# The last 64 contraction rows of two experts: full 128-row products in place of row pairs

## The chip, the cores and the metric

The kernel runs on one core of a Trainium2 chip. The metric is the device time of one execution in microseconds. Three runs of the kernel before gave 1248.62, 1251.45 and 1251.56 us, so its median is 1251.45 us.

## The reference, cut to what matters

A recurrent attention (4 batches, 8 heads, 768 steps, width 40) feeds two experts over 3072 tokens of width 320. All of it is float32:

```python
x = attn_out.transpose(0, 2, 1, 3).reshape(B * S, H * D)      # 3072 x 320
h = x @ w_in                                                  # 320 -> 2048
x = (h * (1.0 / (1.0 + np.exp(-1.702 * h)))) @ w_out          # 2048 -> 320
a, b = x @ w1, x @ w2                                         # 320 -> 1024, twice
y = ((a * b) @ w3) @ w_out2                                   # 1024 -> 1024 -> 320
```

The contractions over 320 in `x @ w_in`, `x @ w1` and `x @ w2` are what the change is about: 320 is two times 128 and a rest of 64.

## The kernel before, in words

The tensor engine multiplies float32 numbers that are split in a high part and a remainder (the tiles ending in h and l). A product of two such numbers is taken as high times high, high times low and low times high. For the first 256 contraction rows that makes three products of 128 rows for each of two row blocks. For the last 64 rows one tile holds the high parts on one half of the partitions and the low parts on the other half (`wir` and `wr` for the weights; `xt4`, `xt5` and `xtb4`, `xtb5` for the tokens, which hold the halves in opposite order). One full 128-row product of `wir` with the opposite tile gives the two mixed terms at once. The high times high term is a product over 64 rows alone, `wir[r]` with `X(4 + h)[r]`.

So each output tile of 128 features takes eight products: six full ones, one full mixed one and one of 64 rows. The kernel before places the 64-row product of one feature tile last and that of the next one first, on the other half of the partitions and into another PSUM bank, so that two stand next to each other on the engine.

The first expert (`moe1`, 12 blocks of 256 tokens) makes 16 feature tiles per block: line 895 emits the eight products (256 columns each), lines 899 to 902 apply the activation and split the result, and line 876 (in `l2`) emits the six products of 320 columns with the output weights, two feature tiles behind. The second expert (`moe2`, 6 blocks of 512 tokens) makes 8 pairs of feature tiles per block: line 1078 emits two times eight products of 512 columns, lines 1083 to 1087 multiply and split, and line 1061 (in `l4`) emits twelve products of 320 columns. Line 1013 folds w3 into the last output weights beforehand.

The attention (lines 381 to 671) is a chain of small products of 32 to 104 rows with work on VectorE, ScalarE and GpSimd between them. A block of the first expert can start when four groups of the attention are done.

The order of all instructions is made before the kernel runs, by `Plan.run`: a list schedule that takes operations as they become ready, by their `at` (their turn) and an assumed cost. It assumes 0.1095 us for each product of line 895, and 0.2155 us for each of line 1078, whatever their rows. Each engine then runs its list strictly in that order. Products of the experts ("PEw") alternate with those of the attention. In the first expert an extra key, "m1", on the first and last product of each feature tile keeps the two 64-row products adjacent.

Of the kernel before, what the change touches and what calls it, by code (L numbers as in the profile page):

```python
# [9 lines left out]
F32 = mybir.dt.float32  # L10
# [8 lines left out]
C = 64            # chunk length  # L19
NB = 4            # batches  # L20
NP = 4            # head pairs
D = 40
NCH = 12
NG = NCH * NB     # groups: one chunk of one batch
NBLK = 6          # token blocks of two chunks
TB = 512
DM = 320
# of a group, per head: the whole chunk's product of decays, those to the chunk's end, those from its start, a, b
# [4 lines left out]
NF = 256          # tokens of a block of the first expert: one chunk  # L33
NLW = 3
NLE = 7           # first loads in the room of the weights to come
NCV = 40 + 20     # tiles of weights taken to float32 before the last expert's output weights
LAG = 2           # its second product runs behind the first
OWN = {"PE": 0.0, "DVE": 0.127, "ACT": 0.13, "Pool": 0.1}     # latency to the next one on the same engine, us
# [34 lines left out]
LE = 4          # first products of a and b emptied by the scalar engine  # L73
JA = 4          # first masked products of a and k left to the others than the vector engine
PMIN = 1e-20       # below 0.5 ** 64: no product of decays within the guards is so small
# [7 lines left out]
class Bank:  # L83
    """A PSUM bank, bound to a tile when its first writer is emitted."""
# [5 lines left out]
class Plan:  # L90
    """Operations in a plain sequential order, emitted in the order of a list schedule.

    Every operation names what it reads and writes; that gives the order that has to
    stay, the rest is free: each engine takes, of what is ready, the operation whose
    turn `at` comes first.
    """
# [40 lines left out]
    def run(self, log=None):  # L137
# [6 lines left out]
        # a bank is taken only when what empties it waits for nothing older  # L144
# [18 lines left out]
        warm, win, act = False, 0, 0.0      # the clock of the tensor engine  # L163
# [69 lines left out]
def rwkv_moe_kernel(ctx: ExitStack, tc: tile.TileContext, LA, JK, JR, KBT, VT,  # L233
# [8 lines left out]
    x2sc = dp.tile([NCH, 2, 128, DM], F32, name="x2sc")    # transposed within blocks of 32 x 32  # L242
    psc = dp.tile([NG, 104, SC], F32, name="psc")
    w12sc = dp.tile([8, 3, 128, 256], F32, name="w12sc")
    G_X = 16 + 4 * NBLK            # columns of GD: inputs, T, x, weights
# [13 lines left out]
    # constants  # L259
# [39 lines left out]
    # ------------------------------------------------------------ turns  # L299
# [14 lines left out]
    # ------------------------------------------------------------ set-up  # L314
# [53 lines left out]
    # ------------------------------------------------------------ attention  # L368
# [17 lines left out]
    def L_part(n):  # L386
        at = at_L(n)
        if n < NLE:           # the first ones in the room of the weights to come
            t, nm = le[n], f"le{n}"
        else:  # L390
            m = (n - NLE) % (NLW + 1) if n < 16 else (n - 16) % NLW
            t, nm = (lw[m], f"lw{m}") if m < NLW else (xsg[0:104, 0:SC + 256], "lx")
# [25 lines left out]
        # what is not below the diagonal is left out later  # L418
# [9 lines left out]
    def T_part(blk):  # L428
# [12 lines left out]
        # all rows for the second diagonal blocks, then the first ones over it  # L441
# [6 lines left out]
        def upper():  # L448
            """Zeros over the diagonal, ones on it; the steps below keep under it."""
            for h in (16, 8, 4, 2, 1):  # L450
                g.memset(bass.AP(LP.tensor, lpf[:, h:].offset, [list(lpf.ap[0]), [66 * h, 16 // h], [32, h], [1, h]]), 0.0)
            g.memset(lpf[:, 0:1024:33], 1.0)
# [15 lines left out]
        # what the merges need first; what the first diagonal blocks' rows get here the merges write over  # L468
# [128 lines left out]
    def S_part(n):  # L597
# [5 lines left out]
        if n >= 4:  # L603
            # the state times all of the chunk's decay, and its transpose
# [73 lines left out]
    # ------------------------------------------------------------ weights  # L678
# [23 lines left out]
    def f64(at, n, srcs):  # L702
        """Tile of float32 from float64 words, all 24 bits; a guard counts the results that are normal."""
# [35 lines left out]
    def split(at, dst_h, dst_l, src, key, kd, n=256, eng="Pool", r=()):  # L739
        """Exact halves of src; kd: key of the result."""  # L740
# [5 lines left out]
    def remainder(at, dst, st, key, kd, h):  # L746
        """High parts of rows 64h to 64h + 63 of st on the same rows of dst, the low parts on the other rows."""
# [44 lines left out]
    # ---- first expert  # L792
    xrc = [0]

    def x_part(blk, at, second):
        """The tokens of a block in exact halves."""
# [63 lines left out]
    def moe1(k):  # L860
# [19 lines left out]
        for f in range(16):  # L880
# [7 lines left out]
            r = slice(64 * h, 64 * h + 64)  # L888
            prods.append((lambda fs=fs: wir[:, fs], lambda h=h: X(5 - h)))
            # half of the rows: next to that of a neighbour, which is on the other rows  # L890
            prods.insert(7 * (f % 2), (lambda fs=fs, r=r: wir[r, fs], lambda h=h, r=r: X(4 + h)[r]))
            for i, (a, b) in enumerate(prods):
                if i == 7 and f % 2 and f >= LAG:
                    l2(f - LAG)
                op("PEw", 0.1095, at(), lambda a=a, b=b, i=i, B=B: mm(B.t[:, 0:NF], a(), b(), start=(i == 0), stop=(i == 7)),  # L895
                   r=ks + [f"wi{f // 2}"], w=[B] + ["m1"] * (i in (0, 7)))
# [7 lines left out]
            if f >= LAG and f % 2 == 0:  # L904
                l2(f - LAG)
# [8 lines left out]
    # ---- second expert  # L914
    order2 = [(k % 2) * 4 + k // 2 for k in range(8)]

    def second_weights():
        """w1 and w2 as float32 in DRAM: piece c, rows k."""
# [122 lines left out]
    def moe2(blk):  # L1041
# [12 lines left out]
        def l4(f):  # L1054
            gi = f % 2
            terms = [(t, z, *("gh gh gl".split()[z], "ph pl ph".split()[z])) for t in range(4) for z in range(3)]
            if f == 7:      # the low parts are the last to come
                terms.sort(key=lambda x: (x[0] // 2, x[1] // 2, x[0]))
# [5 lines left out]
        for f in range(8):  # L1064
            gi = f % 2
            Bs = []
            for m in range(2):
# [5 lines left out]
                prods.append(("wr", None, 5 - m))  # L1073
                prods.insert(7 - 7 * m, ("wr", None, 4 + m))
                r = slice(64 * m, 64 * m + 64)
                for i, (a, k, b) in enumerate(prods):
                    rows = r if k is None and b == 4 + m else slice(0, 128)
                    op("PEw", 0.2155, at(), lambda a=a, k=k, b=b, i=i, B=B, fs=fs, rows=rows: mm(  # L1078
                        B.t, dyn[a][rows, fs] if k is None else dyn[a][:, k, fs], X(b)[rows], start=(i == 0), stop=(i == 7)),
# [13 lines left out]
        for t in range(4):  # L1093
# [6 lines left out]
            q = s if t % 2 and blk == NBLK - 1 else sp       # two queues at the very end  # L1100
# [4 lines left out]
    # ------------------------------------------------------------ input guards  # L1105
    def guards():
        """Decays within (0.5, 1.5), b not large; the first expert's weights make room."""
# [27 lines left out]
    def verdict():  # L1135
        """How many of the guards hold."""
# [13 lines left out]
    # ------------------------------------------------------------ program  # L1150
# [40 lines left out]
    # the general path computes everything again when a guard does not hold  # L1191
# [6 lines left out]
def general_path(ctx: ExitStack, tc, ysc, rr, rk, rv, rw, ra, rb, w_in, w_out, w1, w2, w3t, w_o2, out):  # L1198
    """Step by step over time, then both experts in plain float32: for inputs outside the guards."""
# [82 lines left out]
    # w3 comes transposed: fold it into the output weight, rows of w3 along the free side  # L1282
# [46 lines left out]
def host(inputs):  # L1329
# [3 lines left out]
    def hp(x):  # L1333
        x = x.reshape(NB, NP, 2, NCH, C, D)[:, :, ::-1]
        return x.transpose(2, 5, 3, 0, 1, 4)  # eo e c b hp t
# [6 lines left out]
    def rows(*xs):      # the odd heads on rows 0 to 39, the even ones on rows 64 to 103  # L1342
# [6 lines left out]
    LA[D:64, :, NP * C + 1:2 * NP * C:C] = 2.0 ** -40      # the unused rows fade  # L1349
    JR = f(H["r"])  # L1350

    def tm(x):
        x = x.reshape(NB, NP, 2, NCH, C, D)
        return x.transpose(3, 0, 4, 1, 2, 5).reshape(NG, C, NP, 2, D)  # n s p eo' d (0 = even)
# [6 lines left out]
    VT = v.transpose(0, 1, 3, 2, 4)  # n s eo' p d  # L1361
# [32 lines left out]
```

## Time and profile before

| | |
|---|---|
| median of three runs | 1251.45 us |
| span of the profiled execution | 1251.8 us |
| PE busy | 1078.5 us (86%), 11322 matmuls |
| weight loads (PEld) busy | 915.3 us (73%) |
| DVE, ACT, POOL busy | 818.6, 697.8, 508.8 us |
| mean granted TensorE clock | 0.946 of full speed |
| first and last product of the first expert's input (line 895) | start at 170.9 and 958.9 us |
| last attention product (line 664) | starts at 787.4 us |
| last product of the second expert (line 1061) | starts at 1232.5 us |

The page gives no time of the profiled execution other than its span. Busy time of PE counts a product from its start to its modelled end, and products overlap in the array: a 256-column product lasts about 0.28 us, while the next one starts after about 0.115 us. What a product costs is therefore read from the distance between starts, not from its duration.

### The profile page before, as it was taken

To read this page: it belongs to the slowest core of one execution; us is meant where nothing else is said; L and a number is where in the kernel's file an instruction comes from. 1 tells how busy PE (TensorE), PEld (TensorE's weight loads), DVE (VectorE), ACT (ScalarE), POOL (GpSimd) and SP (SyncE) were. 2 spreads that over 40 slices of the span, in tenths; PEclk is the share of its full clock that TensorE was granted. 3 is DMA by queue.
4 is the path that set the end of the run, shared out by engine and by line. 5 is a ranking of instruction groups with operands and counts; after the bars stand their busy time and mean duration, and the time that the engine had idled before them with its cause. 6 is when DMAs were issued, how large, how long until landed. Compare 5 with 4: busy or idle time off the path is not lost.

```text
span 1251.8 us, 30058 instructions
## 1 busy us (share of the span) xinstructions
PE 1078.5 (86%) x11322; PEld 915.3 (73%) x11322; DVE 818.6 (65%) x1571; ACT 697.8 (56%) x2050; POOL 508.8 (41%) x704
## 2 busy tenths in 40 slices
PE   3355678788997989898998999999999999999993
PEld 3244467676876778777877788999998778878873
DVE  8999999989869996996589323577742233233221
ACT  4345576775675666564755677687754933223121
POOL 4546654766456646543654454454432000000000
PEclk9999978888899989887998999999999999999997
DMA  7537554765476447433632333344324621021000
GB/s 216 147 96 206 150 150 107 187 178 132 121 199 185 122 131 209 124 94 86 159 91 62 90 86 75 85 143 129 121 55 88 224 47 28 19 47 27 4 21 24
DMA packets 187017, 139.71 MB, mean 112 GB/s; under 512 B 123632, under 2 KB 157680, under 8 KB 186864
## 3 DMA queue, kind: packets, MB, share of 16 engines
q1 hardware_dynamic: 186604, 137.38, 41.2%
q8 instruction: 91, 1.49, 0.5%
q14 instruction: 62, 0.51, 0.1%
q10 hardware_dynamic: 260, 0.33, 0.1%
HBM read 107.82 MB, written 29.83 MB: 110 GB/s over the span
## 4 chain that ended last, share of the span: by engine, by line
PE 46%; DVE 3%; DMA 1%; ACT 1%; issue 1%; POOL 0%; SPq 0%; DVEq 0%; POOLq 0%; ACTq 0%
PE bank L1078 15%; PE bank L895 9%; PE bank L876 8%; PE bank L1061 7%; PE bank L1013 2%; PE bank L663 1%; DVE lp L463 1%; PE bank L637 1%; PE bank L648 1%; DVE tmp L459 1%; PE bank L536 1%; DMA lw<-in_LA_dram 0%; DVE lp L443 0%; PE bank L626 0%; DMA pq<-psc 0%
## 5 line engine op out<-in xcount | busy, mean ns | idle before, releaser
L902 POOL TENSOR_TENSOR gl<-xsg,gh 128x256 fp32r<-128x256 f32 x192 | 152.3, 795 | 152.7 <-ACT gh L901 104.1
L895 PE MATMUL bank<-xt,wih 128*128 128x256 f32 x768 | 166.7, 303 | 0.0
L895 PEld LDWEIGHTS bank<-xt,wih 128*128 128x128 f32 x768 | 126.0, 196 | 12.8 <-issue 1.3
L876 PE MATMUL bank<-woh,gh 128*128 128x320 f32 x384 | 125.8, 328 | 3.2 <-DVE xo L911 3.2
L899 ACT ACTIVATE xsg<-bank 128x256 f32<-128x256 f32 x192 | 73.6, 384 | 94.4 <-PE bank L895 91.2
L876 PE MATMUL bank<-woh,gl 128*128 128x320 f32 x384 | 124.6, 325 | 0.0
L876 PE MATMUL bank<-wol,gh 128*128 128x320 f32 x384 | 124.6, 324 | 0.0
L1084 DVE TENSOR_TENSOR sa<-bank,sa 128x512 f32<-128x512 f32 x48 | 33.2, 692 | 138.6 <-PE bank L1078 134.9
L895 PE MATMUL bank<-xt,wil 128*128 128x256 f32 x384 | 112.3, 293 | 0.0
L895 PE MATMUL bank<-xt,wir 64*128 64x256 f32 (+1 forms) x384 | 103.4, 342 | 0.8 <-ACT xsg L899 0.8
L463 DVE TENSOR_TENSOR lp<-lp,tmp 128x30 f32<-128x30 f32 (+9 forms) x180 | 89.1, 495 | 4.3
L574 POOL TENSOR_TENSOR xy<-xy,mup 64x256 f32<-64x256 f32 x96 | 78.9, 822 | 27.8 <-ACT xy L572 20.2
L459 DVE TENSOR_TENSOR tmp<-lp 128x30 f32<-128x30 f32 (+9 forms) x180 | 82.3, 457 | 3.9
L663 PE MATMUL bank<-xy,kb 128*40 128x104 f32 x384 | 56.7, 300 | 27.9 <-DVE xy L654 27.8
L876 PEld LDWEIGHTS bank<-woh,gh 128*128 128x128 f32 x384 | 75.4, 196 | 6.7 <-DVE xo L911 3.6
L901 ACT CAST gh<-xsg 128x256 fp32r<-128x256 f32 x192 | 77.2, 403 | 3.0
L895 PEld LDWEIGHTS bank<-xt,wir 64*128 64x128 f32 (+1 forms) x384 | 61.6, 193 | 23.3 <-issue 17.0
L876 PEld LDWEIGHTS bank<-woh,gl 128*128 128x128 f32 x384 | 75.2, 196 | 3.3 <-issue 1.1
L876 PEld LDWEIGHTS bank<-wol,gh 128*128 128x128 f32 x384 | 75.5, 197 | 2.9 <-issue 0.8
L895 PEld LDWEIGHTS bank<-xt,wil 128*128 128x128 f32 x384 | 75.5, 197 | 1.9 <-issue 0.6
L654 DVE TENSOR_TENSOR xy<-bank,mtx 64x416 f32<-64x416 f32 x96 | 56.4, 587 | 29.4 <-PE bank L649 27.0
L1083 ACT COPY sa<-bank 128x512 f32<-128x512 f32 x48 | 28.2, 587 | 84.8 <-PE bank L1078 84.8
(208 smaller groups left out, 3510.4 us busy)
## 6 DMA issues: line engine op xcount, KB each, us to landing
lw<-in_LA_dram SPq DMA_DIRECT2D x39, 416.0 KB
psc<-lw SPq DMA_DIRECT2D x39, 313.6 KB
pq<-psc SPq DMA_DIRECT2D x48, 209.6 KB
jk<-in_JK_dram SPq DMA_DIRECT2D x48, 208.0 KB
raw<-in_w3t_dram SPq DMA_DIRECT2D x32, 256.0 KB
kb<-in_KBT_dram SPq DMA_DIRECT2D x48, 160.0 KB
raw<-in_w_out_dram SPq DMA_DIRECT2D x20, 256.0 KB
xq<-x2sc SPq DMA_DIRECT2D x72, 64.0 KB
```

The source lines that it names most:

```text
L459: e.tensor_tensor(t, _bc(LP[:, j + 1:32, j:j + 1], [128, n, j]), _bc(LP[:, j:j + 1, 0:j], [128, n, j]), op=ALU.mult)
L463: e.tensor_tensor(LP[:, j + 1:32, 0:j], LP[:, j + 1:32, 0:j], t, op=ALU.add)
L574: op("Pool", 0.69, at, lambda eo=eo, r=r: g.tensor_tensor(xy[r, :, eo, D:104], xy[r, :, eo, D:104], _bc(mup[r], [64, NP, C]), op=ALU.mult) ...
L654: op("DVE", 0.5, at, lambda eo=eo, r=r: v.tensor_tensor(xy[r, :, eo, :], v3(B2, 416)[r], _bc(mtx[r], [64, NP, 104]), op=ALU.mult), r=[B2, ...
L663: mm(ps[64:104, p], kbf[:, 80 * p + 40:80 * p + 80], xy[:, p, 0], start=True, stop=True)
L876: op("PEw", 0.136, at(), lambda w_=w_, g_=g_, z=z, t=t: mm(acc[t].t[:, 0:DM], g_()[:, 128 * t:128 * t + 128], w_(), start=(f == 0 and z == 0),
L895: op("PEw", 0.1095, at(), lambda a=a, b=b, i=i, B=B: mm(B.t[:, 0:NF], a(), b(), start=(i == 0), stop=(i == 7)), r=ks + [f"wi{f // 2}"], w= ...
L899: op("ACT", 0.34, at(), lambda B=B, si=si: s.activation(sg[:, si], B.t[:, 0:NF], AF.Gelu_apprx_sigmoid), r=[B], w=[f"sg{si}"])
L901: op("ACT", 0.305, at(), lambda GH=GH, si=si: s.copy(GH(), sg[:, si]), r=[f"sg{si}"], w=[kg[0]])
L902: op("Pool", 0.69, at(), lambda GH=GH, GL=GL, si=si: g.tensor_tensor(GL(), sg[:, si], GH().bitcast(F32), op=ALU.subtract), r=[f"sg{si}", k ...
L1061: op("PEw", 0.136, at(), lambda a=a, b=b, t=t, ts=ts, z=z: mm(acc[t].t[:, 0:DM], dyn[a][gi][:, ts], dyn[b][:, f], start=(f == 0 and z == 0 ...
L1078: op("PEw", 0.2155, at(), lambda a=a, k=k, b=b, i=i, B=B, fs=fs, rows=rows: mm(B.t, dyn[a][rows, fs] if k is None else dyn[a][:, k, fs], X ...
```

## The change

The 64-row product becomes a product over all 128 rows of the same two tiles. It then also adds low times low on the other 64 rows, which is a term more of the exact product. The two products with `wir` (or `wr`) stand last in every feature tile, none stands first, the "m1" key is gone, and `l2` follows every feature tile instead of standing before the last product of the odd ones. The number of instructions stays the same. Apart from this the diff takes comments away, by which lines move: 895 is now 892, 1013 is 1010, 1061 is 1058, and 1078 is 1072.

```diff
             h = f // 2 % 2
-            r = slice(64 * h, 64 * h + 64)
-            prods.append((lambda fs=fs: wir[:, fs], lambda h=h: X(5 - h)))
-            prods.insert(7 * (f % 2), (lambda fs=fs, r=r: wir[r, fs], lambda h=h, r=r: X(4 + h)[r]))
+            for z in (4 + h, 5 - h):
+                prods.append((lambda fs=fs: wir[:, fs], lambda z=z: X(z)))
             for i, (a, b) in enumerate(prods):
-                if i == 7 and f % 2 and f >= LAG:
-                    l2(f - LAG)
                 op("PEw", 0.1095, at(), lambda a=a, b=b, i=i, B=B: mm(B.t[:, 0:NF], a(), b(), start=(i == 0), stop=(i == 7)),
-                   r=ks + [f"wi{f // 2}"], w=[B] + ["m1"] * (i in (0, 7)))
+                   r=ks + [f"wi{f // 2}"], w=[B])
...
-            if f >= LAG and f % 2 == 0:
+            if f >= LAG:
                 l2(f - LAG)
...
-                prods.append(("wr", None, 5 - m))
-                prods.insert(7 - 7 * m, ("wr", None, 4 + m))
-                r = slice(64 * m, 64 * m + 64)
+                prods += [("wr", None, 4 + m), ("wr", None, 5 - m)]
                 for i, (a, k, b) in enumerate(prods):
-                    rows = r if k is None and b == 4 + m else slice(0, 128)
-                    op("PEw", 0.2155, at(), lambda a=a, k=k, b=b, i=i, B=B, fs=fs, rows=rows: mm(
-                        B.t, dyn[a][rows, fs] if k is None else dyn[a][:, k, fs], X(b)[rows], start=(i == 0), stop=(i == 7)),
+                    op("PEw", 0.2155, at(), lambda a=a, k=k, b=b, i=i, B=B, fs=fs: mm(
+                        B.t, dyn[a][:, fs] if k is None else dyn[a][:, k, fs], X(b), start=(i == 0), stop=(i == 7)),
                        r=ks + [("w2", 4 * m + f // 2)], w=[B])
```

On PE, in the first expert behind the end of the attention, the kernel before has this order from the full mixed product of an odd feature tile (bank 5) to the next tile (bank 4). The sizes are those of the output, so the 64-row products don't show by them: they are the `xt4` product of bank 5 and the `xt5` product of bank 4.

```order
L895 MATMUL bank5_125<-xt5_158,wir_135 128x256
L876 MATMUL bank6_126<-woh_136,gh1_162 128x320
L876 MATMUL bank6_126<-wol_405,gh1_162 128x320
L876 MATMUL bank6_126<-woh_136,gl1_164 128x320
L876 MATMUL bank7_127<-woh_136,gh1_162 128x320
L876 MATMUL bank7_127<-wol_405,gh1_162 128x320
L876 MATMUL bank7_127<-woh_136,gl1_164 128x320
L895 MATMUL bank5_125<-xt4_157,wir_135 128x256
L895 MATMUL bank4_124<-xt5_158,wir_135 128x256
L895 MATMUL bank4_124<-xt0_153,wih_134 128x256
```

In the changed kernel the same place of the program reads:

```order
L892 MATMUL bank5_125<-xt1_154,wil_404 128x256
L892 MATMUL bank5_125<-xt5_158,wir_135 128x256
L892 MATMUL bank5_125<-xt4_157,wir_135 128x256
L876 MATMUL bank6_126<-woh_136,gh0_161 128x320
L876 MATMUL bank6_126<-wol_405,gh0_161 128x320
L876 MATMUL bank6_126<-woh_136,gl0_163 128x320
L876 MATMUL bank7_127<-woh_136,gh0_161 128x320
L876 MATMUL bank7_127<-wol_405,gh0_161 128x320
L876 MATMUL bank7_127<-woh_136,gl0_163 128x320
L892 MATMUL bank4_124<-xt0_153,wih_134 128x256
```

The second product with `wir` moved ahead of the six output products, next to the first, and the next feature tile begins with a full product.

On PE, in the second expert, the kernel before has at the joint of a pair of feature tiles (banks 0 and 2):

```order
L1078 MATMUL bank0_120<-xtb1_11180,w2l_9515 128x512
L1078 MATMUL bank0_120<-xtb5_11184,w2r_9516 128x512
L1078 MATMUL bank0_120<-xtb4_11183,w2r_9516 128x512
L1078 MATMUL bank2_122<-xtb5_11184,w2r_9516 128x512
L1078 MATMUL bank2_122<-xtb0_11179,w2h_9514 128x512
```

The third and fourth rows are the two 64-row products. The changed kernel has there (banks 3 and 0):

```order
L1072 MATMUL bank3_123<-xtb1_11180,w2l_9553 128x512
L1072 MATMUL bank3_123<-xtb4_11183,w2r_9554 128x512
L1072 MATMUL bank3_123<-xtb5_11184,w2r_9554 128x512
L1072 MATMUL bank0_120<-xtb0_11179,w2h_9552 128x512
L1072 MATMUL bank0_120<-xtb2_11181,w2h_9552 128x512
```

The second tile's product with `w2r` left the joint for the end of its own tile.

On PE, right behind the last attention product (line 664), the kernel before goes on with

```order
L664 MATMUL bank3_123<-xy2_94,kb2_97 40x104
L895 MATMUL bank4_124<-xt0_153,wih_134 128x256
L895 MATMUL bank4_124<-xt2_155,wih_134 128x256
L895 MATMUL bank4_124<-xt0_153,wil_404 128x256
L895 MATMUL bank4_124<-xt1_154,wih_134 128x256
```

and the changed kernel with

```order
L664 MATMUL bank1_121<-xy2_94,kb2_97 40x104
L892 MATMUL bank4_124<-xt1_154,wil_404 128x256
L892 MATMUL bank4_124<-xt5_158,wir_135 128x256
L892 MATMUL bank4_124<-xt4_157,wir_135 128x256
L876 MATMUL bank6_126<-woh_136,gh0_161 128x320
```

The first expert's work moved forward against the attention: ahead of the last attention product stand 961 products of line 895 and 708 of line 876 before, and 981 and 720 now, of 1536 and 1152 in all.

## Rows read from the trace of the kernel before

**Rows 1.** Windows, whole core: stretch, length, busy us (count) of PE, PEld, DVE, ACT, POOL; clock, DMA, GB/s

```profile
170.00:577.00 407.00, 351.04 (x4795) 297.94 (x4792) 360.10 (x685) 261.95 (x829) 232.95 (x314) 0.90 0.56 146
577.00:700.00 123.00, 111.78 (x1574) 95.71 (x1574) 86.93 (x166) 71.44 (x225) 61.40 (x88) 0.92 0.40 101
700.00:790.00 90.00, 89.40 (x1242) 77.02 (x1240) 27.97 (x62) 60.96 (x193) 45.26 (x68) 0.98 0.30 74
790.00:960.00 170.00, 170.00 (x1182) 156.82 (x1181) 100.28 (x211) 121.24 (x391) 77.54 (x103) 1.00 0.36 102
960.00:1235.00 275.00, 272.84 (x1359) 217.88 (x1357) 85.65 (x137) 97.31 (x168) 0.74 (x1) 1.00 0.20 55
```

**Rows 2.** Waits of PE, 170 to 700 us, longest: who, for whom, total us, times, longest

```profile
PE bank L663 <- DVE xy L654: 19.8, 8, 4.6
```

**Rows 3.** Timeline of PE, a pair in the first expert: start us, us, engine, instruction, count

```profile
911.23 0.28 PE L895 MATMUL bank<-xt,wih 128*128 128x256 f32 x1
...
911.57 0.31 PE L876 MATMUL bank<-woh,gh 128*128 128x320 f32 x1
...
912.30 0.31 PE L876 MATMUL bank<-woh,gl 128*128 128x320 f32 x1
912.54 0.38 PE L895 MATMUL bank<-xt,wir 64*128 64x256 f32 x2
...
913.19 0.31 PE L1013 MATMUL bank<-foh,f3h 128*128 128x320 f32 x1
```

**Rows 4.** Timeline of PE, a 64-row product alone in the first expert

```profile
929.89 0.31 PE L876 MATMUL bank<-woh,gh 128*128 128x320 f32 x1
930.13 0.38 PE L895 MATMUL bank<-xt,wir 64*128 64x256 f32 x1
930.44 0.41 PE L876 MATMUL bank<-wol,gh 128*128 128x320 f32 x1
930.69 0.31 PE L876 MATMUL bank<-woh,gl 128*128 128x320 f32 x1
```

**Rows 5.** Timeline of PE, a pair in the second expert (the first row merges three products)

```profile
1102.90 0.83 PE L1078 MATMUL bank<-xt,w2r 128*128 128x512 f32 x3
...
1104.23 0.40 PE L1078 MATMUL bank<-xt,w2l 128*128 128x512 f32 x1
...
1104.93 0.39 PE L1078 MATMUL bank<-xt,w2l 128*128 128x512 f32 x1
```

**Rows 6.** Chain that ended last, 1105 to 1112 us: start, us, piece

```profile
1107.33 3.88 PE bank L1078 x16
```

**Rows 7.** Groups of PE by form, 64-row products: 170 to 700, 700 to 790, 790 to 960

```profile
L895 PE MATMUL bank<-xt,wir 64*128 64x256 f32 x99 | 26.5, 400 | 0.8 <-ACT xsg L899 0.8
L895 PE MATMUL bank<-xt,wir 64*128 64x256 f32 x22 | 5.2, 390 | 0.0
L895 PE MATMUL bank<-xt,wir 64*128 64x256 f32 x71 | 16.8, 381 | 0.0
```

**Rows 8.** Windows of line 895 (577, 790), then of line 876: PE, PEld; clock, DMA, GB/s

```profile
577.00:700.00 123.00, 37.95 (x194) 28.67 (x194) 0.92 0.40 101
790.00:960.00 170.00, 90.04 (x564) 73.78 (x562) 1.00 0.36 102
577.00:700.00 123.00, 30.49 (x145) 23.58 (x145) 0.92 0.40 101
790.00:960.00 170.00, 77.18 (x420) 63.43 (x420) 1.00 0.36 102
```

**Rows 9.** Chain that ended last, 577 to 700 us: shares of the stretch by line

```profile
by line: PE bank L895 12.0%; DVE lp L463 8.6%; PE bank L876 8.3%; issue 6.7%; DVE tmp L459 6.0%; DMA lw<-in_LA_dram 4.6%; DVE lp L443 4.4%; DMA pq<-psc 3.7%; DVE ls L475 3.6%; DVE xy L654 3.3%; PE bank L663 3.1%; PE bank L637 2.9%; PE bank 
```

**Rows 10.** Windows, whole core, before and in a stretch at half clock

```profile
570.00:577.00 7.00, 4.57 (x89) 3.83 (x83) 6.91 (x6) 3.88 (x12) 3.31 (x5) 0.93 0.32 84
577.00:600.00 23.00, 23.00 (x293) 20.24 (x294) 8.26 (x20) 11.71 (x35) 7.66 (x12) 0.72 0.37 91
```

**Rows 11.** Waits of ACT, 844 to 930 us

```profile
ACT f3h L976 <- PE bank L1013: 3.9, 3, 1.9
```

## The prediction

> **What bounds the kernel now.** I read the windows first, then the waits and the chain, and last the timeline of PE around the products that change. The windows show two regimes [rows 1]. From 790 to 960 us PE is busy 170.00 of 170.00 us, from 960 to 1235 us 272.84 of 275.00, and from 700 to 790 us 89.40 of 90.00; DVE is busy a third to 60% of these stretches. PE alone sets the pace there, so a microsecond taken from it is a microsecond off the end. From 170 to 700 us PE is idle 56 + 11.2 = 67 us and DVE is busy 84% of the time. PE waits there for the attention, above all line 663 for DVE [rows 2]. In the only part of this stretch that the chain covers, 577 to 700 us, the first expert's products (lines 895 and 876) hold 12.0% + 8.3% = 20.3%, which is 25.0 of 123 us [rows 9]. They are busy for 37.95 + 30.49 = 68.4 us there [rows 8]. So 25.0 / 68.4 = 0.365 of their time lies on the path before 700 us, and all of it afterwards.
>
> **What a pair costs now.** Products are priced by the distance of their starts. Between 911.23 and 911.57 us stand three 256-column products, 0.34 / 3 = 0.114 us each, and from there to 912.30 five of 320 columns, 0.73 / 5 = 0.146 each [rows 3]. The pair of 64-row products starts at 912.54: 0.24 us behind a 320-column product, where 0.146 is normal. From 912.30 to 913.19 there are one 320-column product, the pair and two 256-column ones, 0.89 us. All full they would take 0.146 + 4 x 0.114 = 0.602. So a pair costs 0.29 us more than the two full products that replace it. I take 0.28. The two halves do start together (both lie in one 0.38 us). What is lost is a gap ahead of them and a slow restart behind.
>
> A 64-row product alone is worse. From 929.89 to 930.69 us stand a 320-column product, the single and another 320-column one, 0.80 us. Full they would take 2 x 0.146 + 0.114 = 0.406, so the excess is 0.39 us [rows 4].
>
> In the second expert a full product of 512 columns takes (1104.93 - 1104.23) / 3 = 0.233 us. From 1102.90 to 1104.23 there are a full one, the pair and two full ones, 1.33 us against 5 x 0.233 = 1.167, an excess of 0.16 us [rows 5]. A piece of 16 products with one pair lasts 3.88 against 16 x 0.233 = 3.73, an excess of 0.15 [rows 6]. I take 0.155.
>
> The full product that comes in is not a new price: the mixed product on the same tiles (`wir`, 128 rows) already is one of those three between 911.23 and 911.57 us.
>
> A rule speaks against the change. The Trainium skill (TensorEngine Tiling (Array Packing), Theoretical Speedup) gives up to 2x for a contraction of 64 rows or fewer, since two tiles work at once. By that alone two full products would cost one product more than a pair, and the sum would turn positive (the last rival). The common start of the two halves agrees with it. But the same page says under Key Properties that changing the tiling mode drains the engine, and the gaps around the pair [rows 3 to 5] are what such a drain would look like: 0.28 us lost against 0.114 us won.
>
> **The sum.**
> - 790 to 960 us: 71 products of 64 rows [rows 7]. In the timeline 27 pairs (first at 791.09, last at 955.92 us) and 17 singles make them up: 27 x 0.28 + 17 x 0.39 = 14.2 us. Cross-check by counts [rows 1, 8]: 564 products of 256 columns, 420 + 192 of 320 and 6 of 512 would take 64.3 + 89.4 + 1.4 = 155.1 us in a stretch of 170.0, an excess of 14.9.
> - 700 to 790 us: 22 of them [rows 7], 6 pairs and 2 singles among wide products (2.5 us), and 3 pairs and 2 singles with an attention product on one side, where the array changes its shape anyway. For these I count what is left on the other side, 0.18 and 0.2 us: 0.9. Together 3.4 us.
> - 960 us to the end: 8 pairs in each of 6 blocks; 46 stand as pairs and 4 as singles: 46 x 0.155 + 4 x 0.39 = 8.7 us.
> - 170 to 700 us: 99 of them [rows 7]: 30 pairs and 13 singles among wide products, 4 pairs and 18 singles beside the attention: 13.5 + 4.3 = 17.8 us of PE time. The bounds are 0 (all of it becomes waiting for DVE) and 17.8 (PE sets the pace). I take the share on the chain: 0.365 x 17.8 = 6.5 us.
> - The new order puts 20 products of 256 columns and 12 of 320 more ahead of the last attention product: 20 x 0.114 + 12 x 0.146 = 4.0 us of work that leaves the PE-bound end. It costs nothing where it fills PE's waits, and delays the attention by as much where it lies on the path. The same share gives a gain of 0.635 x 4.0 = 2.5 us, with bounds 0 and 4.0.
> - `l2` behind every feature tile and the freed "m1" key add no instruction and no wait to any other engine or queue; they act by the order alone, which is counted. Activation and splitting keep their work, and DVE has 41% or more and ACT 29% or more to spare where PE is the bound, but for the ACT of rival 4.
>
> After 700 us that is 26.3 us, with the rest 35.3. The profiled span of 1251.8 us (no other time of that execution is given) becomes 1216.5. The median of the runs is 0.35 us below that span, so I predict **1216 us**.
>
> **The rivals.**
> 1. *The time before 700 us gives nothing*: every microsecond that PE saves there is spent waiting for DVE, and the reordering helps nothing. For it: DVE at 84%, PE's waits [rows 1, 2]. Against it: the chain share of 0.365 [rows 9]. 1251.8 - 26.3 = 1225.5 us. Chance 0.18.
> 2. *All of it counts*: PE's queue holds up the attention more than the chain from 577 us shows, and 17.8 + 4.0 us are won there. 1251.8 - 48.1 = 1203.7 us. Chance 0.14.
> 3. *The clock takes part of it back.* Before 700 us the granted clock is 0.90 and 0.92 [rows 1], so about 81 + 20 = 101 us run at 1.2 instead of 2.4 GHz. One such stretch came after PE had been busy for only 4.57 of 7.00 us [rows 10]. More idle time may mean more of them: the 11 us of saving off the path would add a sixth to PE's 67 us of idle time, so 17 us at half clock, 8 us of PE work, some 3 us on the path and at most 8. That is 1219 to 1225 us, chance 0.04. To cancel everything it would take 70 us more at half clock; that is "no change", chance 0.02.
> 4. *The preparation of the second expert's weights becomes the bound* from 844 to 930 us, where line 1013 consumes tiles that ACT, DVE and POOL make. Half of the 14.2 us would turn into waits: 1224 us. Against it: ACT waits there for PE to free a tile, 3.9 us [rows 11], so the preparation is held back by PE. Chance 0.03.
> 5. *Slower: the gaps don't belong to the 64-row products*, but to the joint between two feature tiles, with its new bank. Then they stay, and each pair's second product costs its full 0.114 or 0.233 us: after 700 us 36 x 0.114 + 46 x 0.233 = 14.8, before it 34 x 0.114 x 0.365 = 1.4. That is 1268 us. It decides once a joint keeps more than 0.28 us in the first expert and 0.155 in the second. Against it: the single in rows 4 has the gap on both sides in the middle of a run of output products. Chance 0.03. This is also the time by the skill's 2x rule alone.
>
> **How the numbers follow.** The forecast has 0.56. Faster by over 0.3% (3.8 us, about what a measurement of this kernel can tell from no change) are the forecast and rivals 1, 2, 4 and the mild form of 3: 0.95. Same is 0.02, slower 0.03. The range from 1206 to 1230 us holds the forecast, rivals 1, 4 and the mild 3, and the upper edge leaves 4 us for an attention that the new order delays; rival 2 is partly below it.
>
> **What would show it.** Line 892 follows itself and line 876 without gaps, 0.114 and 0.146 us apart, at every joint; a piece of 16 products of line 1072 lasts 3.73 instead of 3.88 us, and the weight loads' idle time there is gone. The last attention product starts some 4 to 10 us earlier than 787.4, and the distance from it to the end shrinks from 464 to about 437 us. PE's waits before 700 us grow by about 9 to 12 us. If the joints still show 0.24 us entries, the price of a pair was read wrongly; if the distance from 790 us on shrinks as said and the end doesn't follow, the attention was delayed.

## The result and the profile after

The changed kernel takes 1221.4 us (median of 4 runs, 1217.65 to 1223.97) against 1251.51 us before in the same session. The ratio is 0.9767, with a 95% interval of 0.974 to 0.9794: 30 us less. The prediction was 1216 us, with a range from 1206 to 1230.

The page of the changed kernel begins with the span and the busy times of the engines:

```profile
span 1222.2 us, 30059 instructions
PE 1031.5 (84%) x11322; PEld 922.7 (75%) x11322; DVE 820.5 (67%) x1571; ACT 696.9 (57%) x2050; POOL 508.3 (42%) x704
```

The number of products is the same as before. PE is busy for 47 us less, although 288 products now work on twice the rows; the weight loads are busy for 7 us more. The windows, in the columns of [rows 1] and over the same stretches but for the last, which ends with PE's work:

```profile
170.00:577.00 407.00, 339.12 (x4665) 298.07 (x4663) 349.86 (x676) 257.98 (x818) 226.82 (x310) 0.89 0.55 144
577.00:700.00 123.00, 110.48 (x1726) 98.39 (x1726) 97.63 (x175) 78.13 (x244) 63.70 (x93) 0.97 0.44 111
700.00:790.00 90.00, 87.96 (x1280) 79.33 (x1275) 28.07 (x61) 61.88 (x192) 47.20 (x69) 1.00 0.30 73
790.00:960.00 170.00, 169.61 (x1233) 166.33 (x1232) 109.35 (x223) 131.54 (x405) 79.63 (x100) 1.00 0.47 130
960.00:1203.00 243.00, 242.91 (x1255) 212.22 (x1254) 77.73 (x126) 82.12 (x147) 0.00 (x0) 1.00 0.15 42
```

PE is still the bound from 700 us on: it is idle for 2.0, 0.4 and 0.1 us in the last three stretches. From 790 to 960 us it starts 1233 products instead of 1182 [rows 1], in the same 170 us. Before 700 us it now idles 530 - 449.6 = 80.4 us, where it was 67.2. So part of what was saved there became waiting. How much is not firm: a second trace of the changed kernel, taken in the comparison of the orders below, idles 530 - 455.66 = 74.3 us there.

The timeline of PE at a joint of the first expert, which answers to [rows 3]:

```profile
913.12 0.28 PE L892 MATMUL bank<-xt,wil 128*128 128x256 f32 x1
913.23 0.31 PE L876 MATMUL bank<-woh,gl 128*128 128x320 f32 x1
913.38 0.28 PE L892 MATMUL bank<-xt,wir 128*128 128x256 f32 x1
913.49 0.31 PE L876 MATMUL bank<-woh,gh 128*128 128x320 f32 x1
913.64 0.28 PE L892 MATMUL bank<-xt,wir 128*128 128x256 f32 x1
913.75 0.31 PE L876 MATMUL bank<-wol,gh 128*128 128x320 f32 x1
```

Both products with `wir` last 0.28 us like any other, and the next product follows after 0.11 us. The 0.24 us entry and the 0.31 us exit of [rows 3, 4] are gone, even where the two lines alternate product by product. And at a joint of the second expert, which answers to [rows 5]:

```profile
1103.43 0.40 PE L1072 MATMUL bank<-xt,w2l 128*128 128x512 f32 x1
...
1104.13 0.39 PE L1072 MATMUL bank<-xt,w2l 128*128 128x512 f32 x1
1104.36 0.63 PE L1072 MATMUL bank<-xt,w2r 128*128 128x512 f32 x2
1104.83 0.63 PE L1072 MATMUL bank<-xt,w2h 128*128 128x512 f32 x2
```

From 1103.43 to 1104.83 us there are six products, 1.40 / 6 = 0.233 us each, across the joint as well. The weight loads follow each other there without idle time, where they idled 0.37 and 0.25 us around the pair before. In the chain of waits a piece of 16 products now lasts 3.72 us, where [rows 6] had 3.88:

```profile
1108.61 3.72 PE bank L1072 x16
```

Where the time came from can be split at the last attention product (line 664). The row of its line gives durations in ns, then the start of its first and of its last product. The last one started at 787.4 us before:

```profile
L664 PE MATMUL bank<-xy,kb x384: 250/253/396, 90.5 to 784.4; 128*40 128x104 f32 x192
```

From there to the end it was 464.4 us and is 1222.2 - 784.4 = 437.8, so 26.6 us came from behind the attention and 3.0 from before its end. The first number holds in the second trace (26.2 us). The second is less firm: the last attention product starts 4.9 us earlier in the second trace, and 5.5 us earlier in a third one whose program is the same up to the second expert (at 781.9 us, in the run with a 64-row product alone).

### The profile page after: what moved, and what is told of

Its sections match the earlier page's. It is cut to its first block, busy times and chain, and to the rows that moved or that the text cites. A ratio compares the mean times of both kernels' runs of the same rounds, so it can differ in the third digit from the quotient of the medians.

```text
span 1222.2 us, 30059 instructions
## 1 busy us (share of the span) xinstructions
PE 1031.5 (84%) x11322; PEld 922.7 (75%) x11322; DVE 820.5 (67%) x1571; ACT 696.9 (57%) x2050; POOL 508.3 (42%) x704
## 4 chain that ended last, share of the span: by engine, by line
PE 51%; DVE 31%; DMA 6%; issue 6%; ACT 3%; POOL 1%; SPq 1%; DVEq 0%; POOLq 0%; ACTq 0%
PE bank L1072 14%; PE bank L892 9%; PE bank L876 9%; PE bank L1058 7%; DVE lp L463 5%; DVE tmp L459 5%; DMA lw<-in_LA_dram 4%; DVE lp L443 2%; DVE xy L654 2%; PE bank L1010 2%; DVE tt L470 2%; DVE ls L475 1%; DVE st L729 1%; PE bank L663 1%; PE bank L637 1%
## 5 line engine op out<-in xcount | busy, mean ns | idle before, releaser
L892 PEld LDWEIGHTS bank<-xt,wih 128*128 128x128 f32 x768 | 132.8, 199 | 6.7 <-ACT xsg L896 3.9
L892 PE MATMUL bank<-xt,wir 128*128 128x256 f32 x384 | 86.9, 293 | 0.2 <-DVE xt L850 0.2
L574 POOL TENSOR_TENSOR xy<-xy,mup 64x256 f32<-64x256 f32 x96 | 76.8, 800 | 23.6 <-ACT xy L572 16.1
L463 DVE TENSOR_TENSOR lp<-lp,tmp 128x30 f32<-128x30 f32 (+9 forms) x180 | 83.5, 464 | 4.2
L654 DVE TENSOR_TENSOR xy<-bank,mtx 64x416 f32<-64x416 f32 x96 | 56.5, 589 | 26.9 <-PE bank L649 14.5
L588 ACT COPY ivt<-bank 64x208 f32<-64x208 f32 x192 | 62.6, 326 | 20.9 <-PE bank L583 15.0
L1080 ACT CAST gh<-sa 128x512 fp32r<-128x512 f32 x48 | 29.7, 619 | 74.4 <-DVE sa L1078 74.4
L671 POOL TENSOR_TENSOR yh<-yh,pq 104x256 f32<-104x256 f32 x48 | 40.0, 833 | 72.7 <-DVE yh L669 61.4
```

The source lines that it names most:

```text
L463: e.tensor_tensor(LP[:, j + 1:32, 0:j], LP[:, j + 1:32, 0:j], t, op=ALU.add)
L574: op("Pool", 0.69, at, lambda eo=eo, r=r: g.tensor_tensor(xy[r, :, eo, D:104], xy[r, :, eo, D:104], _bc(mup[r], [64, NP, C]), op=ALU.mult) ...
L588: op("ACT", 0.24, at, lambda h=h, d=d: s.copy(ivt[d:d + 64, h // 64::2], B2.t[h:h + 64, 0:208].rearrange("p (a b) -> p a b", a=2)), r=[B2] ...
L654: op("DVE", 0.5, at, lambda eo=eo, r=r: v.tensor_tensor(xy[r, :, eo, :], v3(B2, 416)[r], _bc(mtx[r], [64, NP, 104]), op=ALU.mult), r=[B2, ...
```

## The experiments

All runs have the kernel before beside them on the same chip. My theory: the price lies in the change of the array's shape around each 64-row product. From 700 us on it comes off the end in full, and before that only in part. The rivals were that the gaps belong to the joints between feature tiles, and that the new order made the gain.

### The rows alone, in the old order

The kernel before, every engine's order unchanged, and only the rows raised:

```diff
-            r = slice(64 * h, 64 * h + 64)
+            r = slice(0, 128)
...
-                r = slice(64 * m, 64 * m + 64)
+                r = slice(0, 128)
```

> The kernel before with its own order of instructions on every engine, unchanged, and only the rows of the 64-row products of both experts raised to 128. Theory (the price lies in the change of the array's shape at each 64-row product, and PE sets the pace from 700 us on): 14.2 + 3.4 + 8.7 = 26.3 us less after 700 us, and 0 to 6.5 us less before it: 1219 to 1225 us. Rival (the gaps belong to the joint between feature tiles, and the gain of the change came from its new order): no change, 1248 to 1252 us. What is left between this kernel and the changed one (1221.4 us) is the effect of the new order alone; the prediction had 2.5 us of gain for it.

Measured: 1225.44 us against 1251.34, a ratio of 0.9785 (0.9753 to 0.9817), 26 us less. The rows alone make most of the gain, with the joints and their new banks where they were. In the chain of waits the piece of 16 lasts what it lasts in the changed kernel:

```profile
1107.90 3.72 PE bank L1078 x16
```

The gaps therefore belong to the 64-row products. From the last attention product (785.3 us) to the end of this span (1226.6) it is 441.3 us, 23.1 less than before; the terms behind 790 us had 14.2 + 8.7 = 22.9. The saving ahead of that is small, though 17.8 us of PE time were saved before 700 us. The window from 170 to 700 us shows where it went:

```profile
170.00:700.00 530.00, 444.94 (x6367) 393.41 (x6363) 450.85 (x854) 332.91 (x1053) 292.91 (x401) 0.91 0.52 136
```

PE is busy for 17.9 us less than before in the same stretch (351.04 + 111.78 = 462.8 [rows 1]), with practically the same count of products, 6367 against 6369, and DVE for as long as before. The waits of PE for DVE to empty the first expert's sums grew (the first row is the kernel before, the second this one):

```profile
PE bank L876 <- DVE xo L911: 3.2, 2, 1.6
PE bank L876 <- DVE xo L911: 9.1, 3, 5.2
```

Those for the attention's DVE work at line 663 are longer too, in this trace:

```profile
PE bank L663 <- DVE xy L654: 24.4, 11, 4.9
```

They were 19.8 us before [rows 2]. In a second trace of the same kernel the first wait is 8.2 us and the second 20.9, so the growth at line 663 is not sure.

### The three parts one by one

The same edit, in the first expert's blocks 0 to 5 only (`r = slice(0, 128) if k < 6 else ...`):

> As the first, but full rows only in the first expert's blocks 0 to 5, which run before about 683 us; everything else as before, in the same order. It measures the term of the time before 700 us by itself (17.8 us of PE time). Theory of the prediction (the chain's share, 0.365): 6.5 us less, 1245 us. Rival 1 (all of it turns into waits for DVE): no change, 1251 us. Rival 2 (all of it counts): 1234 us.

Measured: 1248.45 us (12 runs, 1242.78 to 1254.78) against 1251.34, a ratio of 0.9976 (0.9955 to 0.9998): 2.9 us less, and between 0.3 and 5.6 by the interval. It is neither nothing nor the 6.5 us of the prediction, and a third of the full saving at most. Its trace has the last attention product at 778.2 us of 1242.6, so 464.4 us behind it as before: what it saves lies ahead of the attention's end.

In blocks 6 to 11 only:

> As the first, but full rows only in the first expert's blocks 6 to 11, which run from about 683 us on. Theory: 14.2 + 3.4 = 17.6 us less, 1234 us, with the last attention product some 3 us earlier. Rival (joints): no change. Rival (the preparation of the second expert's weights becomes the bound from 844 us on): about 7 us of it missing, 1241 us, and waits of PE for line 978's tiles.

Measured: 1235.83 us, 0.9874 (0.9845 to 0.9903): 15.5 us less, with 17.6 inside the interval (12 to 19 us). The rival of a late preparation would have given 10.6, and PE's waits from 700 to 960 us are these two rows:

```profile
PE bank L895 <- ACT xsg L899: 0.5, 1, 0.5
PE bank L876 <- DVE xo L911: 0.2, 1, 0.2
```

No tile of the preparation (line 978) is among them, so that rival falls. In this trace the last attention product starts at 780.5 us, 6.9 us earlier where 3 were expected (two traces of one kernel differ there by up to 3.6 us, as the comparison of the orders shows), and 1231.4 - 780.5 = 450.9 us stand behind it, 13.5 less than before, where the sum had 14.2.

In the second expert only:

> As the first, but full rows only in the second expert. Theory: 46 pairs at 0.155 and 4 singles at 0.39 us, 8.7 us less, 1242.8 us, and nothing different before 945 us. Rival (joints): no change. Rival (two 64-row products at once are worth one product's time): 46 x 0.233 = 10.7 us more, 1262 us.

Measured: 1242.66 us, 0.9912 (0.988 to 0.9945): 8.7 us less, as the sum had it (7 to 15 us by the interval). Its trace has 1242.4 - 787.9 = 454.5 us behind the last attention product, 9.9 less than before. The rivals (no change, and 10.7 us more) fall. The three parts give 2.9 + 15.5 + 8.7 = 27.1 us, which is what they give together (26) within the intervals.

### A 64-row product alone, away from the joint

The changed kernel, with one of the eight products in each tile of the second expert over 64 rows again:

```diff
                 for i, (a, k, b) in enumerate(prods):
+                    rows = slice(64 * m, 64 * m + 64) if i == 6 else slice(0, 128)
```

(and `rows` used for both operands of the product).

> The changed kernel, but in the second expert the high times high product is over 64 rows again, alone, as the seventh of its tile's eight products, in the middle of the tile and not at a joint: 96 singles. Theory (each change of the array's shape costs): 96 x 0.39 = 37.4 us more than the changed kernel, 1259 us, all of it between 940 us and the end, and gaps of 0.32 us ahead of each. Rival (the gaps belong to the joints between tiles and their new bank): 1221 us.

Measured: 1260.33 us, 1.0062 of the kernel before (1.004 to 1.0084), which is 38.9 us more than the changed kernel. Timeline of PE around one of them (the second row merges the 64-row product with the full one behind it), then the chain's piece of 16 products with two of them:

```profile
1101.93 0.40 PE L1073 MATMUL bank<-xt,w2l 128*128 128x512 f32 x1
1102.26 0.93 PE L1073 MATMUL bank<-xt,w2r 64*128 64x512 f32 x2
1103.02 0.62 PE L1073 MATMUL bank<-xt,w2h 128*128 128x512 f32 x2
```

```profile
1107.19 4.49 PE bank L1073 x16
```

The product enters 0.33 us behind its neighbour instead of 0.233, and it and the next one take 0.76 instead of 0.47. Two singles lengthen the piece by 4.49 - 3.72 = 0.77 us, 0.385 each, in the middle of a tile and in one bank. With 96 of them that is 37 us, more than the whole change won.

So a single takes 0.233 + 0.385 = 0.62 us of PE's time. A pair in the kernel before takes 2 x 0.233 + 0.155 = 0.62 us as well. The second half of a pair costs nothing more; what is paid is the way from 128 rows to 64 and back, once for each single or pair.

The weight loads show where the gaps begin:

```profile
1101.70 0.19 PEld L1073 LDWEIGHTS bank<-xt,w2l 128*128 128x128 f32 x1
1102.26 0.18 PEld L1073 LDWEIGHTS bank<-xt,w2r 64*128 64x128 f32 x1 [0.37 <-issue]
1102.68 0.19 PEld L1073 LDWEIGHTS bank<-xt,w2r 128*128 128x128 f32 x1 [0.24 <-issue]
```

The load for the full product of 1101.93 us starts 0.23 us ahead of it, while the product before still runs. The load for the 64-row product starts with that product, at 1102.26 us. Whether the array has to run empty first, or the load is only not taken ahead where the rows change, these runs don't tell apart.

### The effect of the order

Twice the changed kernel was compared with the rows-only kernel. The second time they ran side by side:

> The changed kernel once more, next to the following one on the same chip. 1221 us. The difference of the two is the effect of the new order alone.

> The kernel before in its own order with full rows in both experts, once more. If the new order gains what the prediction had for it: 2.5 us more than the changed kernel, 1224 us. If it only moves work about: the same as the changed kernel within a microsecond.

Measured: 1219.48 us (0.9747, 0.9716 to 0.9778) and 1225.10 us (0.9806, 0.9773 to 0.9839). The first time it was 1221.4 and 1225.44 us. So the new order is worth 4 to 6 us on top of the rows. The intervals overlap in both sessions, so the times alone don't settle it. The rows of line 664 in the second session, the changed kernel first, help:

```profile
L664 PE MATMUL bank<-xy,kb x384: 250/253/397, 90.5 to 782.5; 128*40 128x104 f32 x192
L664 PE MATMUL bank<-xy,kb x384: 250/253/397, 90.7 to 781.7; 128*40 128x104 f32 x192
```

Their spans are 1220.7 and 1223.0 us. Behind the last attention product the changed kernel has 437.8 and 438.2 us in its two traces, and the rows-only kernel 441.3 us in both. The order is worth 3.1 to 3.5 us there, for 4.0 us of work moved ahead. The attention's end (784.4 and 782.5 us against 785.3 and 781.7) shows no delay that is clear of the difference between two traces of one kernel.

### How much of PE's idle time can be filled

The list schedule of the changed kernel, with other numbers. The first of them has the measured distances as costs:

```diff
-                op("PEw", 0.1095, at(), ...
+                op("PEw", 0.114, at(), ...
```

(0.136 became 0.146 and 0.2155 became 0.233 in the same way.)

> The changed kernel, with the list schedule told the measured distances: 0.114, 0.146 and 0.233 us for products of 256, 320 and 512 columns in place of 0.1095, 0.136 and 0.2155. Its order then has 61 products of line 892 and 48 of line 876 fewer ahead of the last attention product, 61 x 0.114 + 48 x 0.146 = 14 us of work that moves behind it. Theory (0.365 of the experts' work before 700 us lies on the path): attention 5 us earlier, 14 us more behind it, 1230 us. If such work costs the attention nothing: 1235 us. If PE sets the pace of the attention too: 1221 us.

Measured: 1229.55 us, 0.9835 (0.9798 to 0.9873), as the theory gave. But it gave it for the wrong reason, as the row of line 664 shows:

```profile
L664 PE MATMUL bank<-xy,kb x384: 250/253/397, 90.3 to 772.8; 128*40 128x104 f32 x192
```

The attention ends 11.6 us earlier than in the changed kernel (9.7 earlier than in its second trace), not 5, and from there to the end it is 1228.4 - 772.8 = 455.6 us, 17.8 more instead of 14.

The other three change one line:

```diff
-RATIO = 1.25
+RATIO = 1.0
```

> The changed kernel, with RATIO 1.0 in place of 1.25 in the list schedule (the experts get a larger share of PE's turns): 1177 products of line 892 and 865 of line 876 stand ahead of the last attention product, where the changed kernel has 981 and 720. That moves 196 x 0.114 + 145 x 0.146 = 43.5 us of work ahead of it; PE was idle for 82 us from 170 to 790 us. Theory (0.365 of it on the path): the attention ends 16 us later and the end comes 28 us earlier, 1194 us. If PE sets the pace of the attention: 1221 us. If PE's waits take it all: 1178 us.

Measured: 1246.22 us, 0.9965 (0.9948 to 0.9982). The expectation was far off.

```profile
L664 PE MATMUL bank<-xy,kb x384: 250/253/397, 90.4 to 817.7; 128*40 128x104 f32 x192
```

```profile
170.00:790.00 620.00, 537.34 (x7608) 482.30 (x7605) 472.89 (x897) 399.99 (x1260) 342.53 (x475) 0.94 0.49 127
790.00:960.00 170.00, 150.58 (x1203) 141.49 (x1203) 107.05 (x226) 132.75 (x403) 73.78 (x97) 0.94 0.48 141
```

```profile
PE bank L1072 <- ACT xtb L837: 11.7, 2, 11.0
PE bank L1072 <- DVE xtb L849: 5.5, 1, 5.5
```

The attention ends 33.3 us later. PE's idle time from 170 to 790 us is 82.7 us, what it was (80.4 + 2.0). The products that moved ahead did not fill a wait; they moved the attention. And behind it PE waits: from 790 to 960 us it idles 19.4 us, where the second expert now stands ready before its first tokens are (line 837). The granted clock there is 0.94, which is about 20 us at 1.2 GHz. So it is 1246.1 - 817.7 = 428.4 us from the last attention product to the end, only 9.4 less than in the changed kernel, although 43.5 us of work were taken out of that part.

With RATIO 0.8:

> As the one before with RATIO 0.8: 1314 and 966 products ahead of the last attention product, 74 us of work moved. Theory, by the same share: the end 47 us earlier, 1174 us, and PE's waits before 790 us down from 82 to about 35 us. If what is added beyond some point only delays the attention, it is no faster than the one with 1.0.

Measured: 1284.91 us, 1.0261 (1.0244 to 1.0278): the same, and worse. The attention ends 86.0 us later:

```profile
L664 PE MATMUL bank<-xy,kb x384: 250/253/396, 90.3 to 870.4; 128*40 128x104 f32 x192
```

With RATIO 1.4:

> The changed kernel with RATIO 1.4 in place of 1.25: 93 products of line 892 and 68 of line 876 fewer ahead of the last attention product, 20.5 us of work moved behind it. If PE's waits are fixed by the order and an added or removed product before 790 us moves the attention nearly by its own time (as in the runs with 1.0 and with the measured costs, by 0.77 to 0.83 of it): attention 16 us earlier, the end 4 us later, 1225 us. By the chain's share of 0.365: attention 7 us earlier, the end 13 us later, 1234 us.

Measured: 1223.52 us, 0.9774 (0.9729 to 0.9818). The last attention product starts 18.5 us earlier for 20.5 us of work taken from ahead of it, and the time is that of the changed kernel within the intervals (1219.48 us in the same session):

```profile
L664 PE MATMUL bank<-xy,kb x384: 250/253/396, 90.5 to 765.9; 128*40 128x104 f32 x192
```

### Fewer changes between attention and experts

```diff
-HYST = 1.0
+HYST = 2.0
...
-LIM = 1.5
+LIM = 2.5
```

> The changed kernel with HYST 2.0 and LIM 2.5 in place of 1.0 and 1.5: the list goes to and fro between attention and experts 273 times instead of 291. If such a change of the array's shape costs as much as a pair's (0.09 us going in, 0.20 us coming out), 9 round trips are 2.6 us of PE time: 1219 to 1222 us.

Measured: 1242.04 us, 0.9932 (0.991 to 0.9954): 21 us slower than the changed kernel instead of 2 us faster.

```profile
170.00:700.00 530.00, 449.84 (x6180) 398.89 (x6177) 434.21 (x833) 324.98 (x1027) 284.91 (x395) 0.87 0.51 133
```

In the window from 170 to 700 us PE is busy as long as in the changed kernel (449.6), but starts 6180 products instead of 6391, at a granted clock of 0.87. That is about 138 of 530 us at 1.2 GHz, where the changed kernel's 0.89 and 0.97 make 97. Whether longer runs of one kind brought the clock down, or the other order the attention, these runs don't tell apart. The last attention product starts at 799.4 us, 15.0 later than in the changed kernel, and 439.6 us follow, so nearly all of the loss lies ahead of the attention's end. The saving of 9 round trips, if it is there, is buried. Nor does every such change go from 128 rows to fewer: the attention's products have 32 to 128 rows, those of line 664 have 128 (and 40 columns of weights, as its rows above say).

No version tried is faster than the changed kernel.

## Why the prediction was right, and where it was off

- **The price of a pair and of a single: right.** 46 pairs at 0.155 us and 4 singles at 0.39 in the second expert gave 8.7 us; measured 8.7 with the second expert alone. That the two agree to a tenth is luck, since the interval is 7 to 15 us. A single was priced at 0.39 us from one place in the first expert; 96 new ones in the second measured 0.385. Rival 5 (the gaps belong to the joint) is refuted twice: by full rows at unchanged joints, where the gaps vanish, and by 64 rows inside a tile, where they appear. One reading was off: "0.28 us lost against 0.114 us won" counts what was won twice, since 0.28 us is already the difference to two full products. The loss is 0.28 + 0.114 = 0.39 us, the same that a single pays.
- **The rule that spoke against the change.** With rival 5 falls the time that the 2x of the Trainium skill (TensorEngine Tiling (Array Packing), Theoretical Speedup) gives alone. The trace agrees with it in that the two halves run side by side: a pair takes no longer than a single, 0.62 us. The Trainium skill also says (TensorEngine Tiling (Array Packing), Key Properties) that a change of tiling mode drains the engine. The trace agrees with it, without showing the drain itself: the 64-row product starts 0.33 us behind its neighbour instead of 0.233, and it and the next one take 0.76 us instead of 0.47.
- **The time behind the last attention product: right.** The sum had 14.2 + 8.7 + 4.0 = 26.9 us there, and 26.6 and 26.2 were measured. Rival 4 did not come: the weights' preparation kept ahead.
- **The time ahead of it: the step that failed.** The forecast had 3.4 us from 700 to 790 us and 6.5 before, less 1.5 for the work moved ahead, so 8.4 in all; three traces show 3.0, 4.9 and 5.5. "I take the share on the chain: 0.365 x 17.8 = 6.5 us" was mis-sized: by itself this part measured 2.9 us (0.3 to 5.6). The 3.4 us were not measured by themselves. The share came from the 123 us that the chain of the kernel before covered. In the changed kernel the chain covers the whole stretch from 170 us:

```profile
by line: issue 9.5%; DMA lw<-in_LA_dram 8.3%; DVE lp L463 7.9%; DVE tmp L459 7.3%; PE bank L892 6.4%; PE bank L876 5.5%; DVE xy L654 4.5%; DVE lp L443 3.5%; DVE tt L470 2.4%; DVE st L729 2.4%; DVE sh L605 2.4%; DVE xl L547 2.2%; DVE ls L475
by line: DVE lp L463 10.9%; DVE tmp L459 10.6%; issue 9.0%; PE bank L892 8.9%; PE bank L876 7.5%; DMA lw<-in_LA_dram 4.9%; DVE tt L470 4.5%; DVE xy L654 3.9%; DVE ls L475 3.6%; PE bank L415 3.2%; DVE xl L547 2.8%; PE bank L536 2.3%; PE bank
```

  These are the shares of 170 to 577 and of 577 to 700 us. The experts' two lines hold 11.9% of 407 and 16.4% of 123 us, 68.6 us in all. The windows of line 892 and of line 876 in the same two stretches say how long they are busy:

```profile
170.00:577.00 407.00, 109.52 (x599) 93.24 (x599) 0.89 0.55 144
577.00:700.00 123.00, 35.29 (x209) 29.28 (x209) 0.97 0.44 111
170.00:577.00 407.00, 98.33 (x432) 74.16 (x432) 0.89 0.55 144
577.00:700.00 123.00, 34.21 (x161) 25.53 (x161) 0.97 0.44 111
```

  That is 277.4 us, so the share in this trace is 0.25, and 0.25 x 17.8 = 4.4 us lies inside what was measured. But a share from one trace is soft. In the second trace of the changed kernel the same reading gives 16.1% of 407 and 18.3% of 123 us, 88.0 of 283.5 us or 0.31. The run with full rows in the second expert alone, whose program is that of before up to the attention's end, has 13.2% + 10.3% of the 123 us, 28.9 of 70.6 us or 0.41, where 0.365 was read before. So the short stretch is one possible reason for the wrong size, and the scatter between traces another; which it was stays open. The last attention product came 3.0 to 5.5 us earlier, where the text said 4 to 10. PE's waits before 700 grew by 13.2 us in one trace and 7.1 in the other, where it said 9 to 12.
- **The order: the sign was right, the size is 4 to 6 us by the times and 3.1 to 3.5 by the traces, where 2.5 was taken**, about the upper bound of 4.0.
- **The share as a rule for moved work: wrong.** The experiments with other orders were expected by the same share. They showed 0.83, 0.77, 1.16 and 0.90 of the moved time at the attention's end (11.6 of 14, 33.3 of 43.5, 86.0 of 74 and 18.5 of 20.5 us, each against one trace of the changed kernel). A chain's share is read from work that stays in its place, and here it did not price work that is put elsewhere. Why the two differ so much is open: every new list also moves the attention's own instructions.
- **Rival 3, the clock, did not decide.** By the windows' granted clock about 101 us before 700 us were at half clock (1.2 GHz), and 97 are now; the second trace of the changed kernel has 0.88 and 0.96, which makes 108. The difference is within what two traces of one kernel show.

The total of 30 us lies between the forecast (35) and rival 1 (26), and a little nearer to rival 1. The interval of the first comparison (1219 to 1226 us) holds rival 1's 1225.5 us and not the forecast's 1216; that of the second (1215 to 1222 us) holds the forecast and not rival 1. So the total decides neither way. The time lies in the stated range because the range was drawn to hold rival 1 as well, and because too much ahead of the attention's end and too little for the order partly cancel. What the runs bear out is the part behind the attention's end.

## What to carry to other kernels

Price small products by the distance of their starts, over the neighbours on both sides. Two half-height products that start together look cheap by themselves, but here they cost more than two full ones (0.155 us with 512 columns, 0.28 with 256), because the way to 64 rows and back was paid for each pair. Where the missing rows can be filled with something that is right to add, full height is the better form. A saving on an engine counts in full only where that engine never waits. Elsewhere its share of the chain is a rough estimate: here one trace gave 0.25, another 0.31 and the first reading 0.365, and 2.9 of 17.8 us, or 0.16, was measured. And it did not price work that moves.

## What the runs showed that was not expected

Idle time of PE in the attention was not room for the larger moves. With 43.5 us of work moved ahead of the attention's end PE's idle time stayed at 82 us and the attention grew by 33 us; with 20.5 us taken away the attention shrank by 18.5. Only the 4.0 us that the change itself moved ahead came off the end nearly in full (3.1 to 3.5 us), with no clear delay of the attention. A single 64-row product costs as much as two side by side, 0.62 us with 512 columns. That is 0.385 us over one full product, and 0.155 over two.
